# A fused convolution and mixture-of-experts kernel, rebuilt around expert streams in DRAM and rounds of fixed slots

## The chip, the cores and the metric

The kernel runs on one core of one Trainium2 chip. The metric is the device time of one execution in microseconds (us), the median over several runs; lower is better. The profile is of one of these executions. "PE" is TensorE, "PEld" its weight loads, "DVE" VectorE, "ACT" ScalarE, "POOL" GpSimd, "SP" SyncE. "Scatter" means a GpSimd indirect DMA, which writes 112 or 128 rows to row numbers that an on-chip tile holds. An "input scatter" writes token rows to the stream of an expert (tensor xcg_sorted), an "output scatter" writes results to the output. A scatter has "landed" when its rows are written and the engines that wait for it are told so.

## The reference, cut to what matters

```python
# x: 8 x 3584 x 192, weight: 8 heads x 7 taps, 28672 tokens, 8 experts, F = 1024
w = softmax(weight)                                  # per head, over 7 taps
conv[b,s,h,g] = sum_k w[h,k] * x_padded[b,s+k,h,g]   # causal, 24 channels a head
x = conv.reshape(28672, 192)
e_idx  = argmax(x @ w_gate)                          # one expert per token
gate_w = softmax(x @ w_gate)[e_idx]
eom    = sigmoid(x @ w_output_gate)[e_idx]
for e in range(8):
    m = e_idx == e
    out[m] = gate_w[m] * eom[m] * (relu(x[m] @ w1[e]) @ w2[e])
```

## The kernel before: the parts that the change and the argument touch

The tokens go in two halves of four sequences. Each half has a stream in DRAM with a region per expert; all regions are zero-filled first. A routing pass over a sequence (convolution, gates, ranks) scatters each token's row to its place, and an expert pass loads 512 rows transposed, multiplies, and scatters the results to the output.

```python
for h in range(NH):                                   # zero-fill of all regions
    for e in range(E):
        for _r in range(0, NSLOT_USE, _zr):
            nc.gpsimd.dma_start(out=xcg_dram[h][...], in_=zrow_dram)
# ... weights: loaded through staging tiles and cast to fp16, all ahead of the first routing
# routing of one sequence: x transposed on TensorE, then the taps on VectorE
for k in range(1, KW):
    nc.vector.scalar_tensor_tensor(out=accA, in0=a_in, scalar=ch_a[:, k:k + 1],
                                   in1=accA, op0=ALU.mult, op1=ALU.add)
    nc.vector.scalar_tensor_tensor(out=accB[0:DB], in0=b_in, ...)
# ... gate logits, ranks, prefix sums ...
nc.gpsimd.indirect_dma_start(
    out=xcg_dram[half], out_offset=bass.IndirectOffsetOnAxis(
        ap=dstu[:, tau:tau + 1], axis=0), in_=xcgn[:, j, :], in_offset=None)
# expert tile of 512 rows
nc.tensor.matmul(pshs[q], w1a[e][...], xgt[0], start=True, stop=False)        # 128 rows
nc.tensor.matmul(pshs[q], w1b[e][64:64 + DB, ...], xgt[1][64:64 + DB],        # 64 rows
                 start=False, stop=True, tile_position=(64, 0))
# ... relu, second product into psy ...
nc.scalar.copy(out=ysb[:, gs, :], in_=psy[:, 0:D])
nc.gpsimd.indirect_dma_start(
    out=out, out_offset=bass.IndirectOffsetOnAxis(ap=oiu[:, gs:gs + 1], axis=0),
    in_=ysb[:, gs, :], in_offset=None, bounds_check=N - 1, oob_is_err=False)
```

The softmax here doesn't subtract the row's maximum and nothing guards it: scores larger than these inputs give would overflow.

## Time and profile before

| | before |
|---|---|
| runs (us) | 1842.13, 1839.96, 1834.54; median 1839.96 |
| span of the profiled run | 1854.9 us |
| mean granted TensorE clock | 0.673 |
| DMA | 111.53 MB, mean 60 GB/s |

The page divides the span into 40 equal slices (46 us each here). A digit is the busy share of an engine in tenths; PEclk is the granted clock in tenths of full speed.

```profile
PE   0005653533635535885895588767588775776770
...
DVE  0006875665846755527722772571021111111110
...
POOL 6500025344444442653255325615522221222222
PEclk9998555555555555875677567558678777768775
```

No row stays at 8 or 9. VectorE is the busiest engine while only routing runs (slices 5 to 15, counted from 0) and nearly idle in the last 13 slices, and the clock is 0.5 or a mix of 0.5 and 1 nearly everywhere.

### The profile page before, as it was taken

To read this page: it belongs to the slowest core of one execution; us is meant where nothing else is said; L and a number is where in the kernel's file an instruction comes from. 1 tells how busy PE (TensorE), PEld (TensorE's weight loads), DVE (VectorE), ACT (ScalarE), POOL (GpSimd) and SP (SyncE) were. 2 spreads that over 40 slices of the span, in tenths; PEclk is the share of its full clock that TensorE was granted. 3 is DMA by queue.
4 is the path that set the end of the run, shared out by engine and by line. 5 is a ranking of instruction groups with operands and counts; after the bars stand their busy time and mean duration, and the time that the engine had idled before them with its cause. 6 is when DMAs were issued, how large, how long until landed. Compare 5 with 4: busy or idle time off the path is not lost. (4 is left out here: it accounts for less than half of the span.)

```text
span 1854.9 us, 17454 instructions
## 1 busy us (share of the span) xinstructions
PE 1078.9 (58%) x4736; PEld 479.4 (26%) x4736; DVE 754.3 (41%) x2028; ACT 588.7 (32%) x1598; POOL 676.8 (36%) x609
## 2 busy tenths in 40 slices
PE   0005653533635535885895588767588775776770
PEld 0002220210302102432442244223233332333330
DVE  0006875665846755527722772571021111111110
ACT  2223240411512315432642263244233332322330
POOL 6500025344444442653255325615522221222222
PEclk9998555555555555875677567558678777768775
DMA  9932110200201003320321132102132111111110
GB/s 324 362 91 79 30 36 13 73 11 14 69 14 57 28 14 84 68 54 21 81 63 43 33 71 60 46 9 68 42 58 47 40 45 29 41 45 40 42 39 22
DMA packets 174370, 111.53 MB, mean 60 GB/s; under 512 B 123291, under 2 KB 163707, under 8 KB 172446
## 3 DMA queue, kind: packets, MB, share of 16 engines
q1 hardware_dynamic: 150814, 52.13, 12.6%
q0 software_dynamic: 23424, 57.86, 9.2%
q8 instruction: 56, 0.92, 0.2%
q14 instruction: 76, 0.62, 0.1%
HBM read 58.64 MB, written 61.74 MB: 65 GB/s over the span
## 5 line engine op out<-in xcount | busy, mean ns | idle before, releaser
L443 POOL DMA_INDIRECT out_dram<-ysb,oiu x264 | 290.3, 1100 | 621.8 <-DMA out_dram<-ysb,oiu 223.1
L375 POOL DMA_INDIRECT xcg_sorted<-xcgn,dstu x224 | 330.8, 1477 | 510.3 <-issue 205.6
L440 PE MATMUL psy<-w,ht 128*128 128x192 f16 x2112 | 267.3, 297 | 141.7 <-ACT ysb L442 109.7
L432 ACT ACTIVATE ht<-psh 128x512 f16<-128x512 f32 x396 | 224.6, 597 | 276.3 <-PE psh L424 273.7
L440 PEld LDWEIGHTS <-ht 128*128 128x128 f16 x2112 | 226.6, 119 | 190.8 <-issue 155.0
L421 PE MATMUL psh<-xgt,w1a 128*128 128x512 f16 x528 | 216.3, 457 | 79.7 <-DMA xgt<-xcg_sorted 29.7
L434 DVE TENSOR_SCALAR ht<-psh 128x512 f16<-128x512 f32 x132 | 91.1, 690 | 384.9 <-PE psh L424 384.6
L244 DVE SCALAR_TENSOR_TENSOR accA<-stripA,ch_a,accA 128x512 f32<-128x512 f32 x336 | 247.4, 736 | 0.0
L247 DVE SCALAR_TENSOR_TENSOR accB<-stripB,ch_b,accB 64x512 f32<-64x512 f32 x336 | 247.0, 735 | 0.0
L424 PE MATMUL psh<-xgt,w1b 64*128 64x512 f16 x528 | 214.0, 452 | 2.8 <-PEq L454 2.0
L252 PE MATMUL psL<-accA,wgs 128*16 128x512 f32 x112 | 103.9, 1030 | 173.9 <-DVE accA L244 173.0
L217 PE MATMUL psA<-identf,xs 128*128 128x128 f32 x224 | 95.3, 437 | 186.8 <-POOL identf L132 91.7
L442 ACT COPY ysb<-psy 128x192 f32<-128x192 f32 x264 | 69.6, 330 | 283.3 <-DMA out_dram<-ysb,oiu 214.2
L268 ACT CAST xcgn<-psn 128x208 f16<-128x208 f32 x224 | 66.1, 354 | 279.5 <-DMA xcg_sorted<-xcgn,dstu 279.5
L261 PE MATMUL psn<-identf,accA 128*128 128x128 f32 x224 | 70.6, 433 | 125.0 <-ACT xcgn L268 124.7
L269 DVE SCALAR_TENSOR_TENSOR xcgn<-hone,prow 128x2 f16<-128x2 f32 x224 | 30.2, 154 | 228.4 <-ACT xcgn L268 218.1
L414 DVE CAST oiu<-oif 128x4 uint32<-128x4 f32 x66 | 11.3, 172 | 243.0 <-DMA out_dram<-ysb,oiu 242.4
L217 PEld LDWEIGHTS psA<-identf,xs 128*128 128x128 f32 x224 | 42.1, 191 | 234.8 <-POOL identf L132 91.7
L253 PE MATMUL psL<-accB,wgs_b 64*16 64x512 f32 x112 | 102.5, 1015 | 0.0
L261 PEld LDWEIGHTS psn<-identf,accA 128*128 128x128 f32 x224 | 39.6, 197 | 226.6 <-ACT xcgn L268 132.7
L421 PEld LDWEIGHTS <-w1a 128*128 128x128 f16 x528 | 48.5, 105 | 170.4 <-issue 143.5
L255 ACT COPY accB<-psL 16x512 f32<-16x512 f32 x56 | 32.1, 574 | 187.1 <-PE psL L253 186.6
(94 smaller groups left out, 854.4 us busy)
## 6 DMA issues: line engine op xcount, KB each, us to landing
xcg_sorted<-zrow_c POOLq DMA_DIRECT2D x112, 208.0 KB, 5.9
xs<-in_x_dram SPq DMA_DIRECT2D x224, 96.0 KB
stage<-in_moe_w_dram SPq DMA_DIRECT2D x64, 96.0 KB
out_dram<-ysb,oiu POOLq DMA_INDIRECT x264, 2.4
stage<-in_moe_w_dram SPq DMA_DIRECT2D x8, 512.0 KB
xcg_sorted<-xcgn,dstu POOLq DMA_INDIRECT x224, 2.3
xgt<-xcg_sorted SPq DMA_TRANSPOSE x132
stage<-in_moe_w_dram SPq DMA_DIRECT2D x8, 256.0 KB
```

The lines of the kernel that those rows point to most:

```text
L217: nc.tensor.matmul(psA[:, c * 128:(c + 1) * 128], xs[:, 0:DA], identf, is_transpose=True, start=(c == 0), stop=(c == NSUB - 1))
L244: nc.vector.scalar_tensor_tensor(out=accA, in0=a_in, scalar=ch_a[:, k:k + 1], in1=accA, op0=ALU.mult, op1=ALU.add)
L247: nc.vector.scalar_tensor_tensor(out=accB[0:DB], in0=b_in, scalar=ch_b[0:DB, k:k + 1], in1=accB[0:DB], op0=ALU.mult, op1=ALU.add)
L252: nc.tensor.matmul(psL[0:GE, 0:TN], wgs[0:DA], accA, start=True, stop=False)
L253: nc.tensor.matmul(psL[0:GE, 0:TN], wgs_b[0:DB], accB[0:DB], start=False, stop=True)
L261: nc.tensor.matmul(psn[:, 0:DA], accA[:, j * 128:(j + 1) * 128], identf, is_transpose=True, start=True, stop=False)
L375: nc.gpsimd.indirect_dma_start(out=xcg_dram[half], out_offset=bass.IndirectOffsetOnAxis(ap=dstu[:, tau:tau + 1], axis=0), in_=xcgn[:, j, : ...
L421: nc.tensor.matmul(pshs[q], w1a[e][:, (fc0 + q) * 128:(fc0 + q + 1) * 128], xgt[0], start=True, stop=False)
L424: nc.tensor.matmul(pshs[q], w1b[e][64:64 + DB, (fc0 + q) * 128:(fc0 + q + 1) * 128], xgt[1][64:64 + DB], start=False, stop=True, tile_posi ...
L432: nc.scalar.activation(out=ht, in_=pshs[q], func=AF.Relu)
L440: nc.tensor.matmul(psy[:, 0:D], hts[fc][:, gs * 128:(gs + 1) * 128], w2sb[e][fc], start=(fc == 0), stop=(fc == FCH - 1))
L443: nc.gpsimd.indirect_dma_start(out=out, out_offset=bass.IndirectOffsetOnAxis(ap=oiu[:, gs:gs + 1], axis=0), in_=ysb[:, gs, :], in_offset=None,
```

## The change

The intent is to take the convolution off VectorE, to let GpSimd issue its scatters without waiting, and to keep TensorE dense by laying routing and expert work side by side. It is nearly a new kernel. A "unit" is 1792 tokens that are routed together; a "slot" is 512 rows of one expert that are multiplied together; a "round" is eight slots, one of each expert, with the routing of two units between them. The core of the change, cut and in part put in words:

```diff
+    # convolution: one matmul per head, stationary a 118x112 band matrix of the softmaxed taps
+    for h in range(H):
+        nc.tensor.matmul(pc[0:BT, 0:NB * GH], band[0:KI, h, :],
+                         xt[0:KI, :, h * GH:(h + 1) * GH], start=True, stop=True)   # fp32, 384 columns
+        evac(cv[0:BT, :, h * GH:(h + 1) * GH], ...)          # ScalarE and VectorE in turn
-                    nc.vector.scalar_tensor_tensor(out=accA, ...)     # 7 taps on VectorE
+    # x of one unit (16 blocks of 112 tokens, each with its 6 tokens of history)
+    nc.sync.dma_start(xt[0:KI, :, :], src(0, NB, 0))         # KI = 118 partitions
+    # each scatter is declared independent of the others of its kind
+    i = nc.gpsimd.indirect_dma_start(out=xcg, ..., in_=xr[P, c, :], in_offset=None)
+    nodep(i, "scatter", ("scatter", "load", "guard"))
+    i = nc.gpsimd.indirect_dma_start(out=out, ..., in_=self.y[:, j, :], in_offset=None, ...)
+    nodep(i, "out", ("out",))
-    zero-fill of every expert region (24 MB)
+    2 MB of guard rows at the head of each expert's stream
-    nc.tensor.matmul(pshs[q], w1b[e][64:64 + DB, ...], ..., tile_position=(64, 0))  # 64 rows
+    nc.tensor.matmul(pp[:, j, :], self.w(F + fc * 128, 128), self.xb, ...)          # padded to 128 rows
+    py = tile_pool("py", bufs=3)                             # y and oi of a slot
+    for r in range(8):                                       # a round
+        bu, iu = plan(r % 2)                                 # 512 rows of each expert: where from
+        loads = [slot_load(reg(bu[0:1, e:e + 1])) for e in range(E)]    # two transposed loads each
+        fr = chain(front(2 * r + 2), front(2 * r + 3))       # routing of the next two units
+        for e in range(E):
+            s = Slot(loads[e], w_at(e * WE), iu[:, e, :])
+            for q in range(4):
+                s.first(q); drain(fr, 2); prev.second(q); drain(fr, 2)
+            prev = s
+    # what is left after eight rounds: a loop with the expert in a register
```

The order of instructions on TensorE, VectorE, ScalarE and SyncE is fixed as written; GpSimd's order is left to the scheduler.

## The prediction

> **What bounds the kernel now.** I read the page first, then the busy table by stage, then the timeline of GpSimd, then the waits. The page shows no engine near its limit:
>
> ```profile
> PE 1078.9 (58%) x4736; PEld 479.4 (26%) x4736; DVE 754.3 (41%) x2028; ACT 588.7 (32%) x1598; POOL 676.8 (36%) x609
> ...
> L443 POOL DMA_INDIRECT out_dram<-ysb,oiu x264 | 290.3, 1100 | 621.8 <-DMA out_dram<-ysb,oiu 223.1
> L375 POOL DMA_INDIRECT xcg_sorted<-xcgn,dstu x224 | 330.8, 1477 | 510.3 <-issue 205.6
> ```
>
> The two GpSimd groups are busy for 621 us, but idle just ahead of themselves for 1132 us. Together that is 1753 of 1855 us. The timeline of GpSimd in the last stage shows what one of these idle times is:
>
> ```profile
> 1445.51 0.98 POOL L443 DMA_INDIRECT out_dram<-ysb,oiu  x1 [2.15 <-ACT ht L432]
> 1448.65 0.98 POOL L443 DMA_INDIRECT out_dram<-ysb,oiu  x1 [2.15 <-DMA out_dram<-ysb,oiu]
> 1451.83 0.98 POOL L443 DMA_INDIRECT out_dram<-ysb,oiu  x1 [2.20 <-DVE oihi L402]
> 1455.08 0.98 POOL L443 DMA_INDIRECT out_dram<-ysb,oiu  x1 [2.27 <-DMA out_dram<-ysb,oiu]
> 1458.19 0.98 POOL L443 DMA_INDIRECT out_dram<-ysb,oiu  x1 [2.13 <-DMA out_dram<-ysb,oiu]
> ```
>
> The period is 3.1 us: 0.98 us of work and 2.1 to 2.3 us until the indirect DMA before has landed. The releaser named changes, the period does not: every scatter waits for the last one, because all write one DRAM tensor (xcg_sorted, or out) and their rows are not known to be distinct. The scatter of the routing stage has the same shape (starts at 335.56, 338.57, 341.59 us). 488 of them at 3.05 us are 1488 us. The stage table says the same:
>
> ```profile
> 0.00:140.00 140.00, 1.97 (x8) 1.41 (x8) 1.93 (x17) 37.34 (x73) 55.65 (x121) 1.00 0.75 258
> 140.00:250.00 110.00, 68.73 (x256) 27.77 (x256) 88.52 (x197) 43.30 (x139) 0.00 (x0) 0.68 0.21 58
> 250.00:735.00 485.00, 217.56 (x775) 82.91 (x776) 299.91 (x699) 128.06 (x420) 215.09 (x112) 0.50 0.13 36
> 735.00:1245.00 510.00, 380.81 (x1744) 166.63 (x1744) 274.44 (x780) 196.80 (x556) 217.22 (x184) 0.67 0.22 50
> 1245.00:1845.00 600.00, 409.81 (x1954) 200.66 (x1953) 89.49 (x336) 183.24 (x413) 188.79 (x192) 0.74 0.19 44
> ```
>
> (columns: stretch, length, then busy us and count of PE, PEld, DVE, ACT and POOL, granted clock, DMA share, GB/s). From 250 to 1845 us there are 488 indirect DMAs in 1595 us, 3.27 us each; in the last stretch 192 in 600 us, 3.13 us each. So the kernel is 250 us of start (weights, zero-fill of the streams, first routing) and then one chain of GpSimd scatters. TensorE waits for it and runs at a granted clock of 0.5 to 0.74.
>
> **What the Trainium skill says, and whether this trace agrees.**
> 1. "DMA: Bandwidth & Descriptors", section "Anatomy of one DMA — SWDGE (gpsimd) path": a GpSimd DMA has about 2 us of fixed cost, most of it the receipt of the write. The trace agrees: 2.1 to 2.3 us between the end of an issue and the next. A wait per DMA pays it; a queue of independent ones should not.
> 2. "TensorE: Matmul & The Clock Gate", "Part 1: The HAM clock gate": the clock is half until the array has been busy for a window of about 3.4 us. The trace has two clocks only, 0.5 and 1.0. Setting streaming time per 3.4 us window beside the clock: from half it rose only after windows at least 0.8 full (41 times), and from full it was kept after 97 of the 99 windows that were half full or more, and lost after all but 3 of those under that. So it is hard to win and easy to keep.
> 3. "SBUF — State Buffer", section "SBUF: two separate sides", on the port pair that VectorE and GpSimd share: a SWDGE issue is blocked while certain VectorE operations hold the port. The trace agrees in the routing stage: the median issue is 0.98 us, yet some take 3 to 10 us, those lie on top of the SCALAR_TENSOR_TENSOR of L244 and L247, and the mean of L375 is 1477 ns.
>
> **The change, part by part.**
>
> *GpSimd.* All scatters of a kind are declared free of dependence on each other. Their number hardly changes: 16 units of 1792 tokens with 16 scatters (256), and 65 slots with four output scatters (260). Computing the routing from the inputs in the reference, the eight rounds take 64 slots and leave 164 tokens of one expert, so the loop for leftovers runs once (66 tiles before). 516 at 0.98 us, the uncontended median, are 506 us; with some port contention (the 672 SCALAR_TENSOR_TENSOR on two SBUF operands are gone) I take 1.05 us, 540 us, 67 us a round (32 + 32 DMAs). That GpSimd can issue without waiting is seen in the zero-fill, ten back to back at 0.5 us.
>
> *VectorE.* The convolution (494 us in L244 and L247, 54 us in L240 and L241) goes to TensorE. Per unit it gets seven PSUM evictions of about 0.55 us, some seventeen small routing operations of 0.2 to 0.35 us and four scalings of 112x768 (0.9 us): 12 us. Per slot a relu of 128x1024 (about 1.2 us; 690 ns at 512) and two small ones: 1.6 us. Round: 24 + 13 + 2 = 39 us.
>
> *ScalarE.* From 330 ns at 192 columns and 597 at 512 the slope is 0.83 ns a column: 1.03 us at 1024. Per slot three relus and two evictions of 384 columns: 4.1 us. Per unit 4.8 us. Round: 33 + 10 = 43 us.
>
> *TensorE.* Start-to-start intervals of adjacent matmuls in the trace, at full and half clock: 192 columns fp16 82 and 160 ns; 512 columns fp16, 128 rows after 128 rows, 216 to 226 and 402 ns; 512 columns when 128-row and 64-row operands alternate 309 and 540 ns (the weight load is then not hidden); fp32 transpose of 128 columns 110 and 213 ns; fp32 512 columns about 900 ns at half (two clocks a column, so 430 at full). The second half of w1 is now padded to 128 rows with zeros, so the dear alternation goes. Slot at full clock: 16 x 0.22 + 32 x 0.083 + four one-column products (0.3) = 6.5 us; at half 12. Unit at full: eight convolutions of 384 columns fp32 (0.34) 2.7; 24 transposes of 112 columns 2.3; eight gate products of 448 columns 3.1; four transposes 0.4; seventeen rank products about 0.9: 9.4 us. Round: 8 x 6.5 + 2 x 9.4 = 71 us at full clock, 131 at half.
>
> So TensorE becomes the bound of a round, with GpSimd (67 us) just beneath. To the 71 us I add:
> - the round's boundary, where slot 0 needs plan, register and both transposed loads: last relu 1.2, plan 1.6, register load 0.3 plus a little, first transpose issue 1.2, second 2.8 from issue to landing (first use before: 730.8 issued, 733.6 used) = 7 us;
> - one or two windows at half clock after this gap: 5 us;
> - in-order waits inside the front (transposes, gate product, transposes, mask, rank need each other's evictions): about 1 us x 4 a unit, 8 us.
> That is 91 us a round for seven rounds, 637 us; the last round has no front: 52 + 12 = 64 us.
>
> *Start.* Zero-filling 24 MB is gone (2 MB of guard rows stay). But 12.6 MB of weights come through three staging buffers, four tiles an expert, so each expert pays a load after a cast: about 9 us each from landing times of 2 to 6 us, 72 us; ahead of it 25 to 30 us for band, guards and x; behind it the last routing and its 16 scatters, about 25 us. First expert matmul near 125 us (733 before, but that is where half 0 ends).
>
> *End.* One leftover pass, wholly serial: registers, VectorE chain of some 17 operations, load, 12 us of cold matmuls, scatter: 30 us. Drain and last landing 15 us (10 before), last second product 3 us.
>
> Sum: 125 + 637 + 64 + 48 = 874; I say 880 us.
>
> **Rivals.**
> (a) *The scatters still wait for one another*, through semaphores or the queue, in place of the declared dependence. Then 516 x 3.05 = 1574 + 125 + 30 = about 1730 us. Against it: the zero-fill DMAs did overlap. Probability 3%.
> (b) *TensorE stays at half clock*, because the front's fp32 transposes and waits keep it under the 0.8 full window. Round 131 + 7 + 4 = 142, seven of them 994, last 107, together about 1270 us. For it: the routing stage before stood at 0.50 throughout. Against it: 52 of 71 us are dense fp16 matmuls, and a half-filled window keeps the clock. A part of it (half of the round cold) gives 1000 to 1050 us.
> (c) *GpSimd becomes the bound*: if scatters stay at 1477 ns and outputs at 1100, a round has 82 us of GpSimd, still beside 91 us of TensorE; late scatters would lengthen the boundary by up to 10 us: 950 us.
> (d) *Start longer*: weight staging at 18 us an expert adds 70 us: 950 us.
>
> **Range and chances.** The central sum assumes mostly full clock. Misses are more likely upward (b partly, c, d), downward if waits overlap better and the gate products in four column groups run together (0.8 in place of 3.1 us a unit, 37 us in all): 800 us. I take 790 to 1040 us. Faster by over 2% in all but rival (a): 0.97; within 2% 0.02; slower 0.01.
>
> **What would show it.** Right: GpSimd indirect issues about 1 us apart without a wait between; TensorE busy over 75% of each round; granted clock above 0.8 between 130 us and the end; seven repeating rounds of about 91 us with a gap of some 7 us; first expert matmul near 125 us. Wrong: 3 us periods on GpSimd (a), clock near 0.5 (b), TensorE waiting for scatters in mid-round (c), first expert matmul after 180 us (d).

## The result, and the profile after

The changed kernel took 1037.38 us (median of 4 runs, 1036.71 to 1039.99); the kernel before took 1841.05 us beside it. The ratio is 0.564, 95% interval 0.5618 to 0.5661. Ratios here are the mean time of one kernel's runs over that of the other's of the same rounds, so not quite the ratio of the medians.

From the page of the changed kernel, the head and the two GpSimd groups (busy us, mean ns, then idle time just ahead of them):

```profile
span 1035.1 us, 12744 instructions
...
PE 637.4 (62%) x4612; PEld 402.4 (39%) x4612; DVE 324.4 (31%) x786; ACT 348.1 (34%) x503; POOL 524.8 (51%) x528
...
L338 POOL DMA_INDIRECT xcg_sorted<-xrow,du x256 | 257.6, 1006 | 308.2 <-DVE xrow L333 232.9
L439 POOL DMA_INDIRECT out_dram<-y,oi x260 | 257.4, 990 | 192.6 <-issue 72.8
```

The idle time of the two groups fell from 1132 to 501 us, and 233 us of that are waits for routed rows, 147 us of it for the first of all. The slices (26 us each):

```profile
PE   0102303408964996499649955995599469947963
...
POOL 3000006151776277627763776377537754776652
PEclk9999655659996999699869986998699879987986
DMA  1124347323223322342334233423342232114310
```

From slice 9 on a pattern of four slices repeats, seven times: two at 8 or 9, two between 4 and 7. These are the rounds. Ahead of them lie nine slices, 230 us, in which no engine is busy for long; the DMA row begins them with 1 and 1. GpSimd in the second round, from its timeline (start, length, then idle time before it and what ended it):

```profile
408.84 0.94 POOL L338 DMA_INDIRECT xcg_sorted<-xrow,du  x1 [0.31 <-issue]
410.08 0.94 POOL L338 DMA_INDIRECT xcg_sorted<-xrow,du  x1 [0.30 <-issue]
411.33 0.94 POOL L338 DMA_INDIRECT xcg_sorted<-xrow,du  x1 [0.30 <-issue]
412.58 0.94 POOL L338 DMA_INDIRECT xcg_sorted<-xrow,du  x1 [0.30 <-issue]
413.82 0.99 POOL L439 DMA_INDIRECT out_dram<-y,oi  x1 [0.31 <-issue]
```

The period of 3.1 us has become 1.25 us: 0.94 of work and 0.30 of issue, and no DMA is waited for. The two gaps near the end of every round can be seen in ScalarE's and TensorE's timelines of the same round:

```profile
401.43 1.02 ACT L410 ACTIVATE ht<-pp 128x1024 f16<-128x1024 f32 x1 [0.50 <-PE pp L404]
420.80 0.48 ACT L432 COPY y<-pyt 128x384 f32<-128x384 f32 x1 [18.35 <-DMA out_dram<-y,oi]
```

```profile
404.81 0.33 PE L421 MATMUL pyt<-wres,ht 128*128 128x192 f16 x2
422.26 0.59 PE L402 MATMUL pp<-xa,wres 128*128 128x512 f16 x1 [17.12 <-ACT ht L410]
...
436.26 0.61 PE L402 MATMUL pp<-xa,wres 128*128 128x512 f16 x1 [5.55 <-DMA xa<-xcg_sorted]
```

The second gap, 5.55 us, is the boundary of the round. The first, 17.12 us, was not in my sum: ScalarE stands 18.35 us before copying a second product into a y buffer. There are three such buffers, and each is free only when its output scatters have landed; these stand in GpSimd's queue behind the input scatters that the timeline above shows. TensorE stops as ScalarE stops. It happens once in each of the seven rounds (waits: us in total, times, longest):

```profile
ACT y L432 <- DMA out_dram<-y,oi: 124.8, 7, 18.3
```

By stretches (length, then busy us and count of PE, PEld, DVE, ACT, POOL, granted clock, DMA share, GB/s):

```profile
0.00:230.50 230.50, 40.47 (x154) 19.23 (x155) 48.78 (x108) 32.14 (x38) 44.31 (x44) 0.76 0.34 100
...
333.00:436.30 103.30, 76.62 (x571) 49.02 (x572) 36.80 (x90) 40.09 (x60) 63.67 (x65) 0.88 0.33 94
...
1006.80:1035.10 28.30, 10.61 (x52) 5.16 (x51) 1.55 (x3) 4.03 (x5) 5.83 (x6) 0.68 0.06 16
```

So the time is 230.5 us of start, 714 us of seven rounds (230.5 to 944.5, 102 us each), 62.3 us of last round and 28.3 us of leftover loop and drain. In the start, SyncE is held in one issue after another (timeline of its queue):

```profile
1.95 37.96 SPq L90 DMA_DIRECT2D xt<-in_x_dram  x1
39.95 33.60 SPq L194 DMA_DIRECT2D sa<-in_moe_w_dram  x1
```

The x load of the first unit (84 KB, then 1327.5 KB on 118 partitions) had been issued in 0.3 us each just before. The load held for 37.96 us is that of the second unit, 1416 KB on 118 partitions, and while both move the core moves 42 to 44 GB/s. The Trainium skill, "DMA: Bandwidth & Descriptors", the paragraph "How many engines (k)" in the section on why a DMA increments its semaphore by 16, says that a transfer goes to the largest number of engines up to 16 that divides the slowest dimension of both its sides: that is 2 for 118, or 0.125 of 16, and the DMA share of 0.14 (3 to 39 us) fits it. The second run below tests this.

### The profile page after: what moved, and what is told of

Same layout as the page of the kernel before. It is cut to its first block, busy times and chain, and to the rows that moved or that the text cites. A ratio compares the mean times of both kernels' runs of the same rounds, so it can differ in the third digit from the quotient of the medians.

```text
span 1035.1 us, 12744 instructions
## 1 busy us (share of the span) xinstructions
PE 637.4 (62%) x4612; PEld 402.4 (39%) x4612; DVE 324.4 (31%) x786; ACT 348.1 (34%) x503; POOL 524.8 (51%) x528
## 5 line engine op out<-in xcount | busy, mean ns | idle before, releaser
L338 POOL DMA_INDIRECT xcg_sorted<-xrow,du x256 | 257.6, 1006 | 308.2 <-DVE xrow L333 232.9
L439 POOL DMA_INDIRECT out_dram<-y,oi x260 | 257.4, 990 | 192.6 <-issue 72.8
L402 PE MATMUL pp<-xa,wres 128*128 128x512 f16 x520 | 208.7, 401 | 187.6 <-ACT ht L410 116.2
L410 ACT ACTIVATE ht<-pp 128x1024 f16<-128x1024 f32 x195 | 199.6, 1024 | 213.7 <-PE pp L404 213.7
L421 PE MATMUL pyt<-wres,ht 128*128 128x192 f16 (+1 forms) x2080 | 221.4, 250 | 1.1 <-DVE ht L408 1.1
L404 PE MATMUL pp<-xb,wres 128*128 128x512 f16 x520 | 207.8, 400 | 5.8 <-DMA xb<-xcg_sorted 5.8
L232 PE MATMUL pc<-xt,band 118*112 118x384 f32 x256 | 111.6, 559 | 111.2 <-ACT cv L222 64.8
L404 PEld LDWEIGHTS <-wres 128*128 128x128 f16 (+1 forms) x520 | 52.7, 101 | 190.1 <-issue 162.2
L432 ACT COPY y<-pyt 128x384 f32<-128x384 f32 x130 | 62.1, 478 | 188.4 <-DMA out_dram<-y,oi 124.8
L408 DVE TENSOR_SCALAR ht<-pp 128x1024 f16<-128x1024 f32 x65 | 79.4, 1222 | 53.3 <-PE pp L404 53.3
L402 PEld LDWEIGHTS <-wres 128*128 128x128 f16 (+1 forms) x520 | 52.2, 100 | 90.3 <-DMA xa<-xcg_sorted 38.4
## 6 DMA issues: line engine op xcount, KB each, us to landing
xt<-in_x_dram SPq DMA_DIRECT2D x8, 1327.5 KB
```

Of the source, the lines that this page charges most:

```text
L232: nc.tensor.matmul(pc[0:BT, 0:NB * GH], band[0:KI, h, :], xt[0:KI, :, h * GH:(h + 1) * GH], start=True, stop=True)
L338: i = nc.gpsimd.indirect_dma_start(out=xcg, out_offset=bass.IndirectOffsetOnAxis(ap=du[P, kc(c):kc(c) + 1], axis=0), in_=xr[P, c, :], in_o ...
L402: nc.tensor.matmul(pp[:, j, :], self.w(fc * 128, 128), self.xa, start=True, stop=False)
L404: nc.tensor.matmul(pp[:, j, :], self.w(F + fc * 128, 128), self.xb, start=False, stop=True)
L408: nc.vector.tensor_relu(out=ht, in_=pp)
L410: nc.scalar.activation(out=ht, in_=pp, func=AF.Relu)
```

## The experiments

Theory after the result: three things hold the time above my 880 us. They are the x loads on two engines (start), the y buffers (rounds), and GpSimd's period of 1.25 us in place of 1.05 us (rounds). Rivals: the late scatters alone set the round, so that y buffers change nothing; weights, not x, set the start. Twelve runs followed, all with correct results; two of them are the changed kernel unedited, and one repeats another. One finding has to come first, because the first runs cannot be read without it.

### The same program on other chips

`c0_after` is the changed kernel, unedited, run as a control beside the second group of experiments.

> The changed kernel once more, unedited, as the control of the first four experiments: all four were slower than its 1037 us, two of them by far more than any theory had it, with stalls of 5 to 20 us in mid-round in which ScalarE waits for TensorE's semaphore although the matmuls lie 15 us back. If that comes from the edits, this run gives 1037 us again; if from the chip or the way it was built and run, about 1130 to 1210 us.

It took 1212.63 us (1207.82 to 1220.98) on a chip called 5 here, where the kernel before took 1850.01; ratio 0.6579. The kernel before is the same within 1.2% on all five chips (1835.77 to 1856.64 us), the changed one is not. Its waits contain a releaser that the record run does not have at all:

```profile
ACT tt L222 <- remote: 81.9, 9, 11.6
ACT ht L410 <- remote: 79.3, 11, 16.5
DVE tt L224 <- remote: 74.6, 9, 12.8
```

"Remote" stands where no engine's work explains the end of a wait. The timelines of the same stretch, TensorE first, show the pattern:

```profile
400.33 0.60 PE L246 MATMUL pt<-identf,cv 112*128 112x112 f32 x4 [1.49 <-ACT tt L222]
```

```profile
413.72 0.53 ACT L222 COPY tt<-pt 128x448 f32<-128x448 f32 x1 [10.89 <-remote]
```

The four transposes end near 400.9; the copy that needs them starts 12.8 us later, though ScalarE is idle. TensorE tells the other engines that a result is there by incrementing a semaphore, a counter on which they wait. I set every such increment beside the modelled end of its matmul (739 of them). In the record run the longest delay was 0.04 us. In this one 170 were over 0.5 us, the longest 17.8 us, 383 us in sum. (Some increments have no record of their own in this trace and are paired with the next one, so the sum is an upper estimate; the idle times of ScalarE and VectorE above need no such pairing.) They are not spread evenly. Counted by how long GpSimd had been issuing scatters without pause: in the first 2 us 12 of 128 were late, from 5 to 10 us 47 of 109, and from 10 to 20 us 48 of 64. In the record run GpSimd issues for over 40 us without pause and none is late.

`c1_after` is the same program once more, on a third chip (14).

> The changed kernel unedited, a second time, as a control. In the record run it took 1037 us and all 739 TensorE semaphore increments that can be paired arrived within 0.04 us of the modelled end of their matmul; in the control on another chip it took 1212 us and 170 increments arrived over 0.5 us late, 383 us in sum. If the slower form belongs to that chip, this run takes 1037 us; if it belongs to something all my runs share, 1205 to 1220 us again with a sum of late increments between 330 and 430 us.

It took 1040.16 us (1038.77 to 1041.09), ratio 0.5666, and no increment was over 0.04 us late. So the changed kernel has two forms, and which it takes differs between runs on different chips. In all, the eight runs with free scatters on chips 13, 5, 15 and 2 (one of them with at most four under way, one the kernel before with its scatters freed) showed late increments of over 370 us in sum, the single one up to 19.0 us in the changed kernels, and the record run and three kernels on chip 14 showed none but one of 0.67 us. Whether chip or something else of those runs is the cause, and what in the hardware delays the increment, these runs do not say. I call the two the late form and the prompt form. From here on, runs are compared within one form, and it is said where that can't be done. In the late form the round is 125 us, in the prompt form 102.5.

### e1_y8, e2_x16, e3_y8_x16: y buffers and x load

All three ran on chip 13 and are of the late form. `e1_y8` gives the output tiles eight buffers; the weight staging pool is closed first to make room:

```diff
-    py = ctx.enter_context(tc.tile_pool(name="py", bufs=3))
+    early.close()                     # wst, the weight staging pool
+    py = ctx.enter_context(tc.tile_pool(name="py", bufs=8))
```

> Eight output tiles y in place of three (the staging pool of the weights is closed first, for the room). Theory: ScalarE stands still for up to 18 us near the end of each round because the y tile it wants to write still waits for its output scatter, which stands behind 16 input scatters on GpSimd; this delays the plan of the next round. With eight tiles that wait goes, a round shrinks from 103 to about 89 us, and the time from 1037 to about 945 us. Rival (c): the slot loads wait for the last input scatter, or GpSimd at 1.25 us an issue bounds the round anyway; then less than 25 us are saved, and SP waits for the landing of xcg_sorted instead.

`e2_x16` cuts each x load into one of 112 partitions and one of 6:

```diff
-            nc.sync.dma_start(xt[0:KI, :, :], src(0, NB, 0))
+            nc.sync.dma_start(xt[0:BT, :, :], src(0, NB, 0, BT))
+            nc.sync.dma_start(xt[BT:KI, :, :], src(0, NB, BT))
```

> The load of x, 118 partitions, is cut into one of 112 and one of 6 partitions. Theory: 118 partitions go to two of the sixteen DMA engines (44 GB/s in the start), and weights, gate weights and guards queue behind them; with 112 partitions the first expert matmul comes at about 140 in place of 231 us and the time falls to about 945 us. Rival: the start is bound by the staging of the weights through three buffers; then no more than 30 us are saved.

`e3_y8_x16` has both edits.

> Both edits together. If they touch different stretches, the savings add: about 855 us. If GpSimd's issue rate then bounds the rounds (64 issues at 1.25 us are 80 us), a round can't go under 80 us and the time not under 820 us.

Measured: 1211.42 us (ratio 0.6575), 1134.54 us (0.6155) and 1133.16 us (0.6144), against 1212.63 us (0.6579) of the unedited one in the same form on chip 5. The cut x load is worth 78 us, and it is worth it in the start: the first expert matmul comes 80 us earlier (at 153.85 us, 233.69 us in `c0_after`, from the timelines; I had expected 140). The slices of `e2_x16` (28 us each) show why: the DMA row begins with 5 and 6 where it read 1.

```profile
DMA  5677335111531135112531145112431131113210
GB/s 123 170 192 224 81 72 136 42 57 57 128 90 39 49 93 147 32 49 65 121 87 42 50 96 141 31 50 79 115 89 47 46 90 46 32 49 87 71 54 16
```

The cause of most of the long start is thereby shown. The y buffers were worth nothing here. The waits say why that does not settle them: in the late form, with three buffers too, ScalarE's wait for an output DMA at the y copy, 124.8 us in the record run, is not there at all (`c0_after`); waits for late increments stand there instead. The longest that begin with ScalarE in `e1_y8`:

```profile
ACT ht L410 <- remote: 66.9, 7, 17.2
ACT tt L222 <- remote: 66.0, 8, 10.9
```

Together with 30.7 us of the same kind at the y copy itself they are longer than the wait that the buffers would have removed. The question can only be put in the prompt form.

`f1_y8_x16_again` put it, with the kernel of `e3_y8_x16` unchanged, in the hope of a chip with the prompt form.

> The kernel with eight y buffers and the x load cut at 112 partitions, once more, for the case that it falls on a chip where the TensorE increments arrive at once. On chips with late increments it took 1133 us with rounds of 125 us (the unedited one 1212 and 125). Where they arrive at once the unedited one takes 1040 us with rounds of 102.5 us, of which 22.5 us lie between GpSimd's last input scatter and the next round's first expert matmul. Theory (those 22.5 us hold an 18 us stop of ScalarE for a y buffer): rounds of 86 to 92 us and 1040 - 78 - 7x13 = 860 to 890 us. Rival (with the stop gone another wait, late scatters or the late plan, takes its place): rounds still 98 to 103 us and 950 to 965 us. On a chip with late increments: 1133 us again.

It fell on chip 15 and was of the late form: 1132.89 us, ratio 0.6159, rounds of 126 us. It repeats `e3_y8_x16` and says nothing of the y buffers.

### e4_rows64: the padding of w1

The second half of w1 is multiplied with 64 rows again, as before, in the rounds:

```diff
-  self.w(F + fc * 128, 128), self.xb,
+  self.w(F + fc * 128, 128)[0:64], self.xb[0:64],
```

> The second half of w1 read with 64 rows again in place of 128 with zeros (128 in the leftover loop), nothing else. Theory: matmuls that alternate between 128 and 64 rows don't hide their weight loads, 309 in place of 216 ns, so a slot takes 1.5 us more on TensorE; but TensorE isn't what sets the round, so of 65 x 1.5 = 97 us only 20 to 50 us show in the time: about 1070 us. If TensorE is the bound, as I predicted, about 1130 us. If the alternation was not the cause of the 309 ns, the interval stays at 216 ns and the time at 1037 us.

1359.55 us median (1344.06 to 1375.31); two of its four runs count as slow (over 1.5% above the fastest). The two fast ones took 1344.06 and 1353.19 us, ratio 0.7315: 137 us more than the 1211.42 us of `e1_y8` on the same chip, which the unedited kernel equals in this form. Their granted clock is 0.757 and 0.748 where `e1_y8` has 0.80. Rounds grew from 126 to about 142 us, though they can be read only from the profiled run, a slow one. That the alternation makes the interval is shown: in its trace a product starts 309 to 323 ns after the one before at full clock and about 540 ns at half, where the changed kernel has 216 and 427. My figures, 309 less 216 ns on 128 products a round, make about 12 us a round and 95 us for eight, and leave out the clock: 373 of these 1040 products ran at half clock, against 173 in `e1_y8`. At the intervals measured (320 and 540 against 216 and 427 ns) the products take an estimated 415 us in place of 261; the profiled run is 154 us longer. So the padding is worth having and the direction was right; the size was too small in the late form, and this run does not say how it is in the prompt one.

### e5_dep and e6_before_free: the declared independence, taken away and given

`e5_dep` is the changed kernel with the scatters of a kind dependent on each other again:

```diff
-            nodep(i, "scatter", ("scatter", "load", "guard"))
+            nodep(i, "scatter", ("load", "guard"))
-                    nodep(i, "out", ("out",))
```

> The changed kernel with the scatters of a kind dependent on one another again, as before. Theory: 516 scatters at 3.05 us give about 1650 to 1750 us, so without this part the rebuilt kernel gains less than a tenth. If the chain is broken up by the two kinds alternating, 1300 us.

`e6_before_free` is the kernel before with only that independence added:

```diff
+    def _free(i, group):
+        inst = i.ins if hasattr(i, "ins") else i
+        tc.declare_no_dep(inst, group=group, reason="distinct rows of the stream or output")
+        tc.add_to_no_dep_group(group, inst)
-                nc.gpsimd.indirect_dma_start(          # and the same around the output scatter
+                _free(nc.gpsimd.indirect_dma_start(..., f"sc{half}")
```

> The kernel before with nothing changed but the two kinds of indirect scatters declared free of each other (loads of the streams still wait for the scatters). Theory: the 3.1 us period of 488 scatters was its bound; without the wait the period is 1.25 us at most, and the next bound is VectorE's convolution and TensorE: VectorE has 754 us, of which some 600 lie in the routing; I expect about 1150 us (range 1050 to 1350), so that more than half of the gain of the whole change comes from this alone. Rival: the routing stage is bound by VectorE and the expert stage by TensorE at half clock; then no lower than 1450 us.

Both ran on chip 5, beside `c0_after`. `e5_dep` took 1455.45 us (ratio 0.788), 243 us more than the 1212.63 us of the unedited kernel. `e6_before_free` took 1604.92 us (0.8694), 245 us less than the 1850.01 us of the kernel before. So on that chip the independence is worth nearly the same in both kernels, about 245 of the 637 us that the change brings there. But neither pair lies within one form. Counted as above, `e5_dep` has few late increments (47, 68 us in sum), `c0_after` 383 us, and `e6_before_free` 268 of them, 709 us in sum (an upper estimate). The two gains are net of the lateness that came with the freed scatters on that chip. From the 1455 us of `e5_dep` to the 1040 us of `c1_after` it would be 415 us, an estimate across two chips. My 1150 us for `e6_before_free` (range 1050 to 1350) was a clear miss; the rival's "no lower than 1450 us" fits the time. In its last stretch TensorE is busy for 436 of 595 us at a clock of 0.81, and 185 increments are late there:

```profile
1000.00:1595.00 595.00, 436.46 (x2478) 205.55 (x2477) 168.87 (x575) 246.11 (x580) 250.20 (x252) 0.81 0.23 55
```

How much of the miss is TensorE's own work, which I had left out, and how much is lateness, this run does not separate. In `e5_dep` the two kinds alternate, so that one works while the other lands (timeline of GpSimd):

```profile
394.96 0.98 POOL L439 DMA_INDIRECT out_dram<-y,oi  x1 [0.34 <-DMA out_dram<-y,oi]
396.25 0.95 POOL L338 DMA_INDIRECT xcg_sorted<-xrow,du  x1 [0.30 <-DMA xcg_sorted<-xrow,du]
398.10 0.98 POOL L439 DMA_INDIRECT out_dram<-y,oi  x1 [0.91 <-DMA out_dram<-y,oi]
```

Two scatters share a period of 3.14 us. That is why it did not go to the 1730 us of my rival (a): the rows are still waited for, but the two kinds wait side by side.

### e7_depth2, e8_depth4, f2_y8_x16_d4: a limit on the scatters under way

Each scatter waits for the second or fourth one before it of its kind (chip 14, beside `c1_after`):

```diff
+    def lane(kind, i, others):                 # DEPTH groups of a kind, in turn
+        k = nth[kind] % DEPTH
+        nth[kind] += 1
+        nodep(i, f"{kind}{k}", tuple(f"{kind}{m}" for m in range(DEPTH) if m != k) + others)
-            nodep(i, "scatter", ("scatter", "load", "guard"))
+            lane("scatter", i, ("load", "guard"))
-                    nodep(i, "out", ("out",))
+                    lane("out", i, ())
```

> Changed kernel with at most two scatters of each kind under way: each waits for the landing of the second one before it of its kind. Theory (many indirect transfers under way make the TensorE's semaphore increments late): late increments fall from 383 us in sum to under 120 us, as in the run with one at a time (69 us), while GpSimd's period stays between 1.25 and 1.6 us, so the time falls to 1060 to 1130 us if not bound by GpSimd. Rival (lateness has nothing to do with the number under way, only with GpSimd's issuing at all): the sum stays over 300 us and the time is 1210 to 1260 us. Second rival (a landing takes over 2.5 us, so two at a time already throttle): period over 1.6 us, 1250 to 1350 us with few late increments.

> The same with four of each kind under way. If the number under way sets the lateness gradually, a sum of late increments between that of two and 383 us, and a time between; if four are as bad as unlimited, 1200 to 1220 us.

`e7_depth2` took 1151.9 us (0.628), `e8_depth4` 1024.43 us (0.558), `c1_after` 1040.16 us (0.5666). Chip 14 has no late increments, so the question of their cause was not answered there. Something else was. With two under way GpSimd waits again:

```profile
419.62 0.94 POOL L338 DMA_INDIRECT xcg_sorted<-xrow,du  x1 [0.66 <-DMA xcg_sorted<-xrow,du]
423.64 0.94 POOL L338 DMA_INDIRECT xcg_sorted<-xrow,du  x1 [3.08 <-DMA xcg_sorted<-xrow,du]
425.21 0.94 POOL L338 DMA_INDIRECT xcg_sorted<-xrow,du  x1 [0.63 <-DMA xcg_sorted<-xrow,du]
429.31 0.94 POOL L338 DMA_INDIRECT xcg_sorted<-xrow,du  x1 [3.16 <-DMA xcg_sorted<-xrow,du]
```

Two scatters take 5.6 us, so a landing here takes about as long as four issues. Set round by round, from the timelines: in `e7_depth2` the last input scatter of a round ends 114 us after the round's first expert matmul, and the next round begins 4.7 us later, 118.7 us in all. There the scatters set the round, and 4.7 us is what its boundary costs. In `c1_after` the last input scatter ends at 80 us, and the next round begins only 22.6 us later. So in the free kernel the scatters do not set the round: 18 us lie between. They are not the stop for the y buffer itself, but what it has put off. In the round shown above the last input scatter ends at 413.5 us, ScalarE stands from 402.45 to 420.80, and the products and copies that it holds up last until 431.2. An estimate: with the stop gone they would end 18 us earlier, at about 413, with the input scatters, and a round would take about 80 + 4.7 = 85 us. With four under way the scheduler mixes the two kinds more finely on GpSimd (at most 20 output scatters in a row in place of 22, and single ones between the input scatters); the last input scatter ends at 83 to 84 us but the next round begins 16 us later, 100 us in all. This is the fastest kernel measured, 1.5% under the changed one on the same chip: a small difference, though the intervals of the ratios (0.5554 to 0.5607 and 0.564 to 0.5692) do not overlap.

`f2_y8_x16_d4` joins all three edits.

> Eight y buffers, the x load cut at 112 partitions, and at most four scatters of each kind under way. If it falls on a chip where the TensorE increments arrive at once: with four under way alone 1024 us and rounds of 101 us there; theory (ScalarE's stop for a y buffer makes rounds long) rounds of 87 to 93 us and 850 to 890 us; rival (another wait takes its place) rounds of 97 to 103 us and 935 to 955 us. If it falls on a chip with late increments, where the same without the limit took 1133 us with 408 us of lateness in sum: theory (the number under way makes it) under 200 us of lateness and 980 to 1080 us; rival (the number doesn't matter) 350 to 430 us and 1115 to 1150 us.

It fell on chip 2, in the late form: 1117.59 us (1110.55 to 1133.42, the last a slow run), ratio 0.6007, against 0.6144 and 0.6159 without the limit. The lateness was 374 us in sum where 408 and 438 us stood without it. So a limit of four hardly changes the lateness; my theory, that the number under way makes it, fails as far as four. One at a time (`e5_dep`) it nearly went, but there GpSimd never issues for longer than 10 us without pause either, so pauses and number are not told apart. The cause stays open. What this kernel would take in the prompt form was not measured; from 1024 us less 78 us for the x load it would be an estimate of 945 us, less what the y buffers give.

## Why the prediction was right or wrong

The time, 1037 us, lies within the predicted 790 to 1040 us, at its very edge; the centre, 880 us, was 157 us too low. The direction and its main reason were right. That it still fell inside is partly luck: the upper end needed rounds that run half at the low clock (1000 to 1050 us), which did not come, as rivals (c) and (d) reach only 950 us; the stop that lengthened the rounds is nowhere in my sum; and in the late form the same kernel takes 1212 us, far outside. Point by point:

1. **GpSimd stops waiting: right; one chain of all scatters: wrong.** The idle time before an issue went from 2.15 to 0.30 us. `e5_dep` and `e6_before_free` show that this alone is worth 243 and 245 us on one chip, lateness included; the other 392 us there come from the rest of the rebuild. But only scatters of one kind wait for each other. In the trace before, 112 of the 487 gaps between scatters are 0.30 us, all of them between scatters of different kinds (86 lie between 735 and 1245 us). Of the 1132 us of idle time, 163 us are ahead of the first scatter, 317 us are 39 gaps of 3 us or more, and only 540 us are the 248 gaps of 1.5 to 3 us, the size that a landing leaves. So my 488 x 3.05 counted too much, and so did the 1730 us of rival (a).
2. **GpSimd's cost of a scatter: too small.** I took 1.05 us of issue and left out the 0.30 us between issues, though the trace before shows it, in the 112 gaps named above. The period is 1.25 us, a round's 64 scatters take 80 us, not 67.
3. **TensorE's work in a round: nearly right, by errors that nearly cancel; that it bounds the round: wrong.** The busy time is 75 to 77 us (0.74 of a round), I said 71. The expert products fit (216 and 82 ns). A convolution product takes two records of 323 ns, 0.65 us, where I said 0.34: I had read fp32 columns off records of which each matmul has two. The Trainium skill, "FP8 and Floating Point Precision", section "TensorE Precision Notes", gives true fp32 four passes; 384 columns in four passes at the rate of the fp16 products (512 columns in 216 ns) are an estimate of 0.65 us, and the trace agrees. The gate products' four column groups did run together (starts 7 ns apart), about 1.5 us for my 3.1.
4. **The round: 91 us predicted, 102 measured; the failed term is missing from the sum.** The boundary (7 us, measured 5.55) was in order. In the round of 103.3 us, TensorE's 76.6 us, the stop of 17.1 and the boundary leave 4 us, where I had 13 for half clock (part of which now lies in the 76.6) and for waits inside the front; so the missing term shows as 11 us and not as 18. The wait for a y buffer, some 18 us a round (124.8 us in seven), is nowhere in it. I had compared sums of busy time (71 and 67 us) and not asked in which order GpSimd's queue holds the two kinds of scatter, nor how many results three buffers can hold meanwhile. Rival (c) and its sign (TensorE waits for scatters in mid-round) had the right engine and the wrong path: not late input scatters but late output scatters. `c1_after` beside `e7_depth2` shows that the input scatters leave 18 us of a round unused; that more buffers recover them is argued and not shown, since the three kernels with eight buffers all fell on chips of the late form.
5. **The start: 125 us predicted, 230.5 measured; the largest error.** This is my rival (d) by its sign (first expert matmul after 180 us), but not in cause. I had taken 25 to 30 us for band, guards and x. SyncE is held for 38 us by an x load and for 34 us more by the weight load behind it, while the loads on 118 partitions move at a DMA share of 0.14. `e2_x16` shows it: 78 us back. With it the first expert matmul still comes 29 us after my 125 us; what makes these was not looked into.
6. **Last round and end.** 64 us predicted, 62.3 measured; 48 predicted, 28.3 measured. That the leftover pass overlaps the drain more than I allowed is likely and was not looked into.
7. **Clock: right.** 0.88 in the rounds and 0.854 over all; rival (b) did not come.

In sum: +105.5 (start) + 77 (seven rounds) - 1.7 - 19.7 = +161 on the 874 of the sum, which gives the 1035 us of the span.

## What to carry to other kernels

When a change frees an engine from waiting, lay out the order of its queue next: what stands behind what, and how many buffers bridge it, is not in the sum of its busy time, and here it stopped ScalarE for 18 us a round. Count partitions before a large load: 118 and 112 + 6 are the same bytes and not the same time. And run a control of the unedited kernel beside experiments: here the same program took 1040 us on one chip and 1212 us on another, while the kernel before was within 1% on both.

## What the Trainium skill lacked or had wrong

- "Perfetto Trace Analysis", section "Tensor Engine Instruction (MATMUL, LD_WEIGHTS)", names the last steps of a matmul (the semaphore update is pushed, then seen by all engines) without a duration. With free scatters on chips 13, 5, 15 and 2 the increment came up to 19.0 us after the modelled end in the changed kernels (`e1_y8`), mostly while GpSimd issued scatters without pause (in `c0_after` 48 of 64 were over 0.5 us late after 10 to 20 us of it); in the record run and in `c1_after` at most 0.04 us. No page has a delay of this size.
- "DMA: Bandwidth & Descriptors", section "Anatomy of one DMA — SWDGE (gpsimd) path", gives one DMA about 2 us of fixed cost, which fits single scatters here (2.15 us of wait). For a queue of independent scatters it has no period: 1.25 us here, 0.94 of issue and 0.30 between; and with two of a kind under way two took 5.6 us.
- The same page, "How many engines (k)", holds: 118 partitions moved 42 to 44 GB/s; cut into 112 and 6 they began at 123 GB/s. It gives no time for how long the issuing queue is held meanwhile: 37.96 us on SyncE.
- "TensorE: Matmul & The Clock Gate" has no time for 128-row and 64-row operands in turn: 309 to 323 ns for 512 columns at full clock against 216 ns with the rows padded to 128; `e4_rows64` cost 137 us.
